# A gated recurrence followed by a low-rank mixer: 11 of ScalarE's 22 transfers go back to SyncE, and all loads and stores get new places

## The chip, the core and the metric

The kernel runs on one core of a Trainium2 chip. The core has TensorE (PE: matrix multiplications), VectorE (DVE), ScalarE (ACT), GpSimd (POOL) and SyncE (SP, which here only issues transfers). Transfers between the chip's memory and the core's on-chip memory run on 16 DMA engines; they are issued by SyncE or by ScalarE, each of which has a queue of its own. The metric is the device time of one execution in microseconds.

## What is computed

There are four batches (b), eight heads (h), 768 tokens (t) and 48 values per head (d). The first stage is a recurrence with a gate for each row of a 48 x 48 state:

```
state = zeros((B, H, D, D))
for t in range(S):
    state = alpha[:, :, t, :, None] * state + einsum('bhd,bhe->bhde', k[:, :, t], v[:, :, t])
    y[:, :, t] = einsum('bhd,bhde->bhe', q[:, :, t], state)
```

The heads of y are put side by side (8 x 48 = 384 columns), which gives x. The second stage mixes x over the tokens by a product of rank 32, adds, and goes through two layers with 1536 hidden values:

```
h  = xt @ U @ V                       # xt: tokens last
u  = x + h.transpose(0, 2, 1)
ch = maximum(u @ w_ch1, 0.0) @ w_ch2
return u + ch
```

Inputs and output are float32.

## The kernel before

**Tiling.** Each batch is worked in six chunks of 128 tokens; "1.2" is chunk 2 of batch 1. A recurrence over a chunk is turned into products: the logarithm of alpha (ScalarE, lines 378 and 549), its running sum (TensorE, 387 to 394 and 556 to 558), the exponentials of that sum and of its negative (ScalarE, 401 to 403, 566 to 569: `aa`, `ai`, `tot`), k and q multiplied by them (GpSimd or VectorE, 409 and 577, into `rkq`), both transposed (TensorE, 426 and 590, evicted into `kqt`), scores, a mask on VectorE (461, 628, into `pm`), a state product that is added to the running state (`st`, VectorE 499, 513, GpSimd 652), and y (TensorE 523 to 533, 680 and 685). v is cast to bf16 into `rv` by the helper of lines 274 to 280, on ScalarE (276), VectorE (278) or GpSimd (280). In batch 3 the transposes of k and q are DMA transposes (602), issued like a load.

The mixer of a batch follows its six chunks: the product with U (700), with V (714), the addition (VectorE, 715), transposes of u (TensorE 734, or DMA transposes 720 for batches 2 and 3), the first layer (763, 288 matmuls of 384 columns over the kernel) with its relu on ScalarE (773) or VectorE (775) into `h1t`, the second layer (789), the last addition (VectorE, 795) and the stores (798 for halves, 800 for the rest). While TensorE works on one batch's layers, the chunks of the next are prepared beside it.

**Loads.** The four inputs of a chunk go into four of 40 buffers `io`. The six chunks of batch 0 and the first four of batch 1 are loaded in token pairs: a transfer (line 348) brings 256 tokens of four heads in rows of 384 bytes. All other chunks are loaded whole (line 355): 128 tokens of eight heads in rows of 192 bytes. Both move 192 KB. The weights come as seven transfers (line 318) into the second half of the hidden layer's buffers, and are cast from there to bf16 (`w_sb`, 276 and 280).

**The order.** Every operation is recorded in a plan as a function with its buffers. Then two strings decide everything: `TABLE` has three characters for each operation, two for its number and one for the engine (P, A, D, G, or S for SyncE), and the operations are issued in that order; "++" stands for a number of matmuls that only keep TensorE busy. `SLOTS` has one character for each buffer that is taken, and names which of its pool it is. Each engine goes through its own operations strictly in this order. For a load, a DMA transpose or a store, the letter picks the queue:

```
def queue(eng):
    return nc.scalar if eng == "ACT" else nc.sync
```

A transfer also takes the next of eight completion lanes (DMAHW0 to DMAHW7 in turn, whichever engine issues it), and its engine waits before it until the transfer eight places earlier in the table has landed. This wait stands in the issuing engine's own order: what comes behind it there, computing or issuing, waits too.

Of the kernel before, what the change touches and what calls it, by code (L numbers as in the profile page):

```python
# [29 lines left out]
B1SJyABtSBqSJEPB5SBmSJFAIgPKKGJ2GI1AI+PI-AKIAIyPI4PKsAI5AIzAJGPIhDI6PI7AJ0AJzAImPIqPKHAIrAInAKaAJKPIwPKDGJ+PJHAIkPKbAKuP  # L30
BoSKwAJIPLDPJLDKcAKMPJ-DLWAJAPJJAIuPKyAJBAKfGIlDKeDKvAIxDKJGLGAI2PI3DLHAIvAIcPLEALIGIdAIePIfAKgPKiDJ3PBxSIoPJ5DLFAIpANFA
KxAIsPKhPItAJ4PKODKjAKSPKTDKLPJSPJTPJ6DK0GCISJ7PLJGKNAKUGKtGB-ACDSJ9DKkPKlDKPPKRDJUPLYPBuSLZANHPKmDNJANKAKYGFqPFrPNNGKzG
LKPCHSI8PNLAJ8DNIAKQDKnPB3ABySB7ALaALcGKqPLMALLPB6SLbDKoDKpGLNAFsPK2PLdPK4DI9AKVPFtDK8PLfAK9DKrAJCPJDAK1PK3DLePNMGLgAK+G
KAPKWANOSCEAJkPCASKBDJVDNWALOPLPDK5PK6DLhPOMAJlPB2SLQDK7DLCGLRPLSDLTGJmPCBSNYPOOPORALXAN6ANbANoANcAJePLjDLUPLiDNaAK-PLAD
LVDJpPLkPJfPLlACCSNZANPPB4ANeGLmPLnAN8PN9ANGGN-ANQDJqPLvPLtPN+ANRDOAANdGJrPLwDOQALqPLuDLxSLrDNXAOeALoPJYPLpDJMPLsSB+SNSP
NTDJgPJZPL0PL1DNfSB8ACFAJhDJsDJaPNqPNtALyPLzDL2SJbDJNPJOPNsAJnDJPDOUGNjPNkDN7AL5PMNPNUPL6ANVDL3PNrAMDPMEAB9SNvDMOAL4ANlG
MFPOBDL9PMHPMIAOPAL-PMAAOCDODSNuAMGAOgPOhAL+AMLPMJPMKDMBPOTGOiANwDMbPMTPCJAMUAL7PJRSMcDNxSMfPMPPMCAMgDNpAMMAMVPMWDMXPMYD
OHPOSAOEPMhPOFDOjGL8DMjPMkAN1PN2DOVSOGDCGAOkGMdPMRPCKSMSDMZPMQDMeDMnPN3GOIDOKPOlSOJGMoPMiAOWPJQSOLANyPMaAFuSOXDNgPNzDFpS
JoSNhDFoSJXSNAPNBPMpPONAN0DOZPJcSOmPNiDN4PM2POaDM3PGASOYDN5AOcPOdANmPMlPObGOnDOfGOoDNnDOpPOqAMxPOrPOsAMyPMqDMmDM4PO3PO4D
OyPO5PO0PO1DM7POtPNCPOzDM8PM9PF1SM5DO6DOuDJdSO2SO7SMzPM+DOvPOwDMsPMtPMuPPiPNDDPkPFvSPoPPpAPaPPbAPcPPWPPXDPdDM0DOxSPMPPNA  # L40
PCPM6SPDDPlAPgPJtSPjAPePPAPJjSPGPPhDPOPPYPPBANESPKPPLDPSPPTAPUPPVDMvDO8PF6SMrSO9APEPPPDPHAPqPPrDPIPO+PJiSPZAQFPPfDQGPGBS
QKPM1SM-SF7SPmPP7PJWSP8PPnDFjSMwSQLPF0SPFAFiSO-DPxPQHPPJDPQPPRDP2PP3PP4PP5DP6SQMPQNDQOSPsPPyPPzPQIDQJSP0DP1SPtPP9PP+DPuP
QAPQBPPvDQCPP-SPwSQDDQES
# [811 lines left out]
```

## Time and profile before

| | |
|---|---|
| median of 3 runs | 159.58 us (159.46 to 161.48) |
| the profiled execution | 159.54 us |
| its span, first instruction to last | 157.6 us |
| TensorE busy | 147.8 us (94%) |
| VectorE busy | 107.9 us (68%) |
| ScalarE busy | 90.2 us (57%) |
| GpSimd busy | 61.5 us (39%) |
| moved by DMA | 31.63 MB, mean 201 GB/s |
| transfers issued by ScalarE | 22: 7 of k, 5 of v, 5 of q, 4 of alpha, 1 of weights |
| TensorE's granted clock | full in all 40 slices |

Times in the profile count from the start of the span, in microseconds. A row of a timeline has start, busy time, engine, line, operation, what it writes <- what it reads, shapes, and the number of like instructions in a row; in brackets stands how long its engine was idle before it, and what ended that. ACTq and SPq are the issuing of transfers by ScalarE and SyncE: such a row's length is what the issue took, not the transfer. DMA in the chain of waits is the time from an issue to its landing. Tile names lose their numbers in the profile. What TensorE's share of 94% hides is where its idle time lies; that is read by stretch.

### The profile page before, as it was taken

The page shows a single profiled execution, that of the slowest core. Times are in us where ns is not written, and L with a number is a line of the kernel's source. Part 1 is how long each engine was busy: PE and PEld are TensorE (multiplying, and loading weights), DVE is VectorE, ACT ScalarE, POOL GpSimd, SP SyncE. Part 2 cuts the span into 40 slices and gives each one's busy share as a digit, 9 for nine tenths or more (in the row PEclk, how much of TensorE's full clock was granted, in tenths as well). Part 3 has the DMA queues.
Part 4 walks back from the last instruction along what each step waited for, and adds up shares of the span by engine and source line. Part 5 has one row for each costly group of instructions (what it writes and reads, how often), then busy time and mean ns, then how long its engine had stood idle before and what let it go on. Part 6 is the DMA issues. An engine that isn't in the chain of part 4 may idle for free.

```text
span 157.6 us, 4405 instructions
## 1 busy us (share of the span) xinstructions
PE 147.8 (94%) x1712; PEld 97.4 (62%) x1712; DVE 107.9 (68%) x236; ACT 90.2 (57%) x233; POOL 61.5 (39%) x95
## 2 busy tenths in 40 slices
PE   0798999998999999999999999999999999999992
PEld 0376677764766656656768666666667555666561
DVE  6029999978899538916587987875989480673162
ACT  3698799986778263999947585279232202450000
POOL 8276993556375550046578343225323000000000
PEclk9999999999999999999999999999999999999999
DMA  5999999998999999999999999979866248842044
GB/s 131 311 319 322 319 227 261 367 251 218 245 339 195 271 176 216 185 190 207 192 217 223 167 196 224 128 157 187 160 123 187 67 85 209 268 132 59 0 152 147
DMA packets 99091, 31.63 MB, mean 201 GB/s; under 512 B 92768, under 2 KB 99040, under 8 KB 99072
## 3 DMA queue, kind: packets, MB, share of 16 engines
q1 hardware_dynamic: 81312, 26.45, 74.8%
q10 hardware_dynamic: 17760, 4.92, 13.9%
q8 instruction: 13, 0.21, 0.6%
q14 instruction: 6, 0.05, 0.1%
HBM read 23.89 MB, written 4.72 MB: 181 GB/s over the span
## 4 chain that ended last, share of the span: by engine, by line
PE 83%; DMA 8%; DVE 5%; ACT 2%; issue 0%; SPq 0%; DVEq 0%
PE ps L789 30%; PE ps L763 30%; DMA io<-in_alpha_dram 5%; DMA io<-in_v_dram 3%; PE ps L714 3%; PE ps L618 3%; PE ps L590 2%; PE ps L685 2%; PE ps L556 2%; DVE pm L461 2%; PE ps L734 1%; PE ps L680 1%; PE ps L641 1%; PE ps L533 1%; PE ps L426 1%; DVE rkq L409 1%
## 5 line engine op out<-in xcount | busy, mean ns | idle before, releaser
L789 PE MATMUL ps<-w_sb,h1t 128*128 128x384 bf16 (+2 forms) x300 | 53.1, 319 | 0.0
L763 PE MATMUL ps<-uT,w_sb 128*128 128x384 bf16 x288 | 51.0, 326 | 0.1
L773 ACT ACTIVATE h1t<-ps 128x384 bf16<-128x384 f32 x58 | 27.2, 509 | 19.0 <-PE ps L763 18.8
L763 PEld LDWEIGHTS <-w_sb 128*128 128x128 bf16 x288 | 27.0, 98 | 16.4 <-issue 0.2
L789 PEld LDWEIGHTS <-h1t 128*128 128x128 bf16 x300 | 27.3, 97 | 15.9 <-issue 0.6
L775 DVE TENSOR_SCALAR h1t<-ps 128x384 bf16<-128x384 f32 x38 | 20.1, 553 | 20.1 <-PE ps L763 20.0
L628 DVE TENSOR_TENSOR pm<-ps,maskc 128x512 bf16<-128x512 f32 x28 | 17.7, 684 | 2.8 <-PE ps L618 2.8
L577 POOL TENSOR_TENSOR rkq<-io,aa 128x384 bf16<-128x384 f32 x12 | 11.3, 949 | 20.4 <-ACT h1t L773 12.1
L715 DVE TENSOR_TENSOR ub<-xb,ps 128x384 bf16<-128x384 bf16 x24 | 12.3, 550 | 6.8 <-PE ps L714 6.8
L795 DVE TENSOR_TENSOR io<-ub,ps 128x384 f32<-128x384 bf16 (+2 forms) x25 | 12.9, 533 | 3.7 <-PE ps L789 3.6
L276 ACT CAST xb<-ps 128x192 bf16<-128x192 f32 (+1 forms) x21 | 8.4, 399 | 10.5 <-PE ps L685 8.2
L461 DVE TENSOR_TENSOR pm<-ps,maskp 128x512 bf16<-128x512 f32 x20 | 13.2, 682 | 0.4 <-ACT ai L401 0.2
L652 POOL TENSOR_TENSOR st<-sm,tot 128x384 bf16<-128x384 f32 x8 | 6.6, 829 | 12.0 <-DVE sm L668 12.0
L577 POOL TENSOR_TENSOR rkq<-io,ai 128x384 bf16<-128x384 f32 x9 | 8.5, 945 | 6.7 <-ACT ai L566 3.8
L409 POOL TENSOR_TENSOR rkq<-io,ai 128x384 bf16<-128x384 f32 x9 | 9.0, 1006 | 5.4 <-ACT ai L401 3.8
L276 ACT COPY kqt<-ps 128x512 bf16<-128x512 bf16 x18 | 10.4, 610 | 1.1 <-PE ps L426 1.1
L566 ACT ACTIVATE ai<-ps 128x384 bf16<-128x384 f32 x14 | 7.0, 502 | 4.3 <-PE ps L556 2.5
L280 POOL CAST w_sb<-h1t 128x384 bf16<-128x384 f32 x14 | 7.1, 528 | 5.3 <-DMA h1t<-in_moe_w_ch_dram 5.3
L278 DVE COPY kqt<-ps 128x512 bf16<-128x512 bf16 x18 | 7.4, 418 | 1.9 <-PE ps L590 1.2
L569 ACT ACTIVATE tot<-ps,off 128x4 f32<-128x4 f32 x22 | 5.6, 279 | 5.2 <-PE ps L558 3.4
L387 PE MATMUL ps<-lt,upto 128*128 128x384 bf16 x10 | 3.6, 363 | 5.2 <-ACT lt L378 5.1
L409 POOL TENSOR_TENSOR rkq<-io,aa 128x384 bf16<-128x384 f32 x7 | 6.7, 957 | 4.1 <-DMA io<-in_q_dram 4.1
(108 smaller groups left out, 225.5 us busy)
## 6 DMA issues: line engine op xcount, KB each, us to landing
io<-in_alpha_dram SPq DMA_DIRECT2D x20, 192.0 KB, 4.6
io<-in_v_dram SPq DMA_DIRECT2D x19, 192.0 KB, 4.8
io<-in_q_dram SPq DMA_DIRECT2D x19, 192.0 KB, 4.3
io<-in_k_dram SPq DMA_DIRECT2D x17, 192.0 KB, 4.4
out_dram<-io SPq DMA_DIRECT2D x13, 192.0 KB, 2.0
h1t<-in_moe_w_ch_dram SPq DMA_DIRECT2D x4, 576.0 KB, 7.5
out_dram<-io SPq DMA_DIRECT2D x20, 96.0 KB, 2.2
h1t<-in_moe_w_ch_dram SPq DMA_DIRECT2D x2, 768.0 KB, 7.1
```

Of the source, the lines that this page charges most:

```text
L276: nc.scalar.copy(dst, src)
L278: nc.vector.tensor_copy(dst, src)
L409: eng.tensor_tensor(jh(dst()[:, :, 0:D]), raw(a), jh(x()), op=ALU.mult)
L461: nc.vector.tensor_tensor(dst, s2, maskp.to_broadcast([C, 2, 2, C]), op=ALU.mult)
L577: eng.tensor_tensor(dst()[:, :, 0:D], a(), x(), op=ALU.mult)
L628: nc.vector.tensor_tensor(pm()[:, :, par, :], s2, maskc.to_broadcast([C, HP, C]), op=ALU.mult)
L715: P.add(f"u {b}.{c}", lambda e, c=c, hb=hb: nc.vector.tensor_tensor(ub()[:, c, :], xb()[:, c, :], hb()[:, 0:DM], op=ALU.add), r=[hb] + xk( ...
L763: nc.tensor.matmul(hb()[:, 0:TW], lhsT=w1_sb[:, ct, jt * 128 : (jt + 1) * 128], rhs=u_half(uT, ct, tt, b in QUEUE_U), start=(ct == 0), sto ...
L773: nc.scalar.activation(dst, hb()[:, 0:TW], AF.Relu)
L775: nc.vector.tensor_scalar_max(dst, hb()[:, 0:TW], 0.0)
L789: nc.tensor.matmul(hb()[:, 0 : hi - lo], lhsT=h1()[:, jt, c * C : (c + 1) * C], rhs=w2_sb[:, jt, lo:hi], start=(jt == 0), stop=(jt == NJ - 1),
L795: P.add(f"out_{hi - lo} {b}.{c}", lambda e, hb=hb, lo=lo, hi=hi: nc.vector.tensor_tensor(flat(ou)[:, lo:hi], ub()[:, c, lo:hi], hb()[:, 0 ...
```

## The change

Only the two strings differ. Their first lines, before and after:

```diff
 TABLE = """
-ArSABSAvAA3SA-SQPAAySAsACLAAtSAwSCNPAzSAuACOACPA++BCiADSA++BECA++BCRGCSG++BAxSBDSCjABASCQAA4A++BCkPClACmAA7S++BDUPDVAA5S
+ArAABSAvSA-AA3SQPAAySAsSCLACNPAtSAzAA5ACOACPAAwS++BCiADSA++BECAAxS++BBAACRGAuSCSG++BCjACQA++BCkPA4SClACmA++BA7ADUPDVADWA
...
 SLOTS = """
-ABCDEFAGHAIJAABCAAKLAMANBBBOCCPCQBDRBEASBFAGHACBBDTCUAEBCBVBDGWAEACDBCGXEBAYDCACZBGAFaBHACAEbCCCFDCBHDCcdDBeBAfGgDAhHFDD
+ABCDEFAAGHIAAJBCAKLAMAABNBBOCCCPBDBEAQBFARSGHACBBDTCUAEBCBVBDGAWEACXDBCEGABDCACBEAFAYZHACAFCCCaGDCAHDCbcDdBAAefghEDAGHDD
...
```

The computing operations stand in the same order on TensorE, VectorE, ScalarE and GpSimd, on the same engines. The 154 transfers stand in another order, and fall differently on the two queues: ScalarE issued 22 and now issues 11, all of them token-pair loads (alpha of 0.0, 0.5, 0.2 and 0.4, q of 0.3 and 0.4, k of 0.5, 1.0 and 1.3, v of 0.5 and 1.3); SyncE issued 132 and now issues 143. Buffers of `io`, `rkq`, `kqt` and banks are dealt out anew.

ScalarE at its start, before. `lt` is a logarithm (of 0.0, 0.1, 0.3 and 0.5 in this order), `ai` and `aa` are exponentials (of 0.0, then 0.1), `rv0_173<-io4_137` is the cast of 0.1's v, the transfers are 0.0's v and 0.3's k:

```order
L378 ACTIVATE lt0_76<-io0_133 128x8x48
L348 DMA io9_142<-in_v_dram 128x4x96
L401 ACTIVATE ai0_181<-ps_212 128x384
L402 ACTIVATE aa0_178<-ps_212 128x384
L378 ACTIVATE lt1_77<-io1_134 128x8x48
L378 ACTIVATE lt2_78<-io2_135 128x8x48
L378 ACTIVATE lt0_76<-io3_136 128x8x48
L276 CAST rv0_173<-io4_137 128x384
L403 ACTIVATE tot0_184<-ps_212 128x8
L348 DMA io13_146<-in_k_dram 128x4x96
L401 ACTIVATE ai1_182<-ps_212 128x384
L402 ACTIVATE aa1_179<-ps_212 128x384
```

The same place after; the transfers are 0.2's alpha, 0.3's q and, ahead of the cast, 0.5's k:

```order
L378 ACTIVATE lt0_76<-io0_133 128x8x48
L348 DMA io7_140<-in_alpha_dram 128x4x96
L348 DMA io8_141<-in_q_dram 128x4x96
L401 ACTIVATE ai0_181<-ps_212 128x384
L402 ACTIVATE aa0_178<-ps_212 128x384
L378 ACTIVATE lt1_77<-io1_134 128x8x48
L378 ACTIVATE lt2_78<-io3_136 128x8x48
L378 ACTIVATE lt0_76<-io2_135 128x8x48
L348 DMA io11_144<-in_k_dram 128x4x96
L276 CAST rv0_173<-io4_137 128x384
L403 ACTIVATE tot0_184<-ps_212 128x8
L401 ACTIVATE ai1_182<-ps_212 128x384
```

Before, 0.3's k took a lane that no one waited for; after, 0.5's k takes the lane of 0.2's alpha, eight places earlier in the table, and so stands on ScalarE behind that landing and ahead of the cast. The load of 0.4's alpha, on SyncE before, comes on ScalarE directly behind the second exponential of 0.1 (`aa1_179`).

SyncE around the first weights, before: the q of 1.2 (`io34`), k and q of 1.3 (`io35`, `io36`), and the k of 1.2 (`io37`):

```order
L318 DMA h1t1_74<-in_moe_w_ch1_dram 128x3x384 x2
L348 DMA io34_167<-in_q_dram 128x4x96
L318 DMA h1t1_74<-in_moe_w_ch1_dram 128x3x384
L348 DMA io35_168<-in_k_dram 128x4x96
L348 DMA io36_169<-in_q_dram 128x4x96
L348 DMA io37_170<-in_k_dram 128x4x96
L355 DMA io39_172<-in_alpha_dram 128x8x48
L318 DMA h1t1_74<-in_moe_w_ch1_dram 128x3x384
```

After: the k of 1.2 (`io34`) is the first behind the two weights, and the q of 1.2 and 1.3 (`io36`, `io37`) come behind the third weight and 1.4's alpha:

```order
L318 DMA h1t1_74<-in_moe_w_ch1_dram 128x3x384 x2
L348 DMA io34_167<-in_k_dram 128x4x96
L318 DMA h1t1_74<-in_moe_w_ch1_dram 128x3x384
L355 DMA io35_168<-in_alpha_dram 128x8x48
L348 DMA io36_169<-in_q_dram 128x4x96
L348 DMA io37_170<-in_q_dram 128x4x96
L318 DMA h1t1_74<-in_moe_w_ch1_dram 128x3x384
```

The k of 1.3 went to ScalarE, the v of 1.2 from ScalarE to SyncE, behind the last of these rows.

SyncE in batch 3, before: `io17` and `io24` are v and q of 3.2, `io35` is v of 3.5; L602 are the DMA transposes of chunks 3.1, 3.3, 3.2, 3.4 and 3.5 in this order, L720 those of batch 2's u:

```order
L720 DMA_TRANSPOSE uT2_211<-ub2_206 128x6x128 x2
L355 DMA io17_150<-in_v_dram 128x8x48
L602 DMA_TRANSPOSE kqt3_191<-rkq3_82 128x8x128
L720 DMA_TRANSPOSE uT2_211<-ub2_206 128x6x128
L355 DMA io24_157<-in_q_dram 128x8x48
L602 DMA_TRANSPOSE kqt1_189<-rkq1_80 128x8x128
L798 DMA out_0_dram<-io21_154 64x384
L602 DMA_TRANSPOSE kqt2_190<-rkq2_81 128x8x128
L602 DMA_TRANSPOSE kqt0_188<-rkq0_79 128x8x128
L355 DMA io35_168<-in_v_dram 128x8x48
L602 DMA_TRANSPOSE kqt1_189<-rkq3_82 128x8x128
```

After, from the last transpose of batch 2's u on: q and v of 3.2, the transposes of 3.3 and 3.4, q of 3.5, the transposes of 3.1 and 3.2, v of 3.4, the transpose of 3.5, a store, v of 3.5:

```order
L720 DMA_TRANSPOSE uT2_211<-ub2_206 128x6x128
L355 DMA io31_164<-in_q_dram 128x8x48
L355 DMA io32_165<-in_v_dram 128x8x48
L602 DMA_TRANSPOSE kqt3_191<-rkq1_80 128x8x128
L602 DMA_TRANSPOSE kqt1_189<-rkq0_79 128x8x128
L355 DMA io13_146<-in_q_dram 128x8x48
L602 DMA_TRANSPOSE kqt2_190<-rkq3_82 128x8x128
L602 DMA_TRANSPOSE kqt0_188<-rkq2_81 128x8x128
L355 DMA io23_156<-in_v_dram 128x8x48
L602 DMA_TRANSPOSE kqt3_191<-rkq1_80 128x8x128
L798 DMA out_0_dram<-io17_150 64x384
L355 DMA io36_169<-in_v_dram 128x8x48
```

The transposes of 3.1 and 3.2 went behind those of 3.3 and 3.4, the v of 3.5 behind the transpose of its own chunk, and q of 3.5 and v of 3.4, which ScalarE issued, stand among them.

More of the change, by code (lines that the diff above doesn't have):

```diff
@@ L52 @@
+aFBGCBCCAeFAGCCBFEEDBCAGABAAdEHDABfADGCgCEFBDhiHkACCGFECDAABmDHClnDDADGCEFBAACBCADBFGCCjAAHDABCBEFBAAGCDACCEDCBFHEFGHJBG
+CACEDBFAABBBDGEKBACMDBCADCBAFBBDDFAGAEACOBFBLCADIPCCAGBFDAQVGecDCGZSfgCUhACABAGBAAHCFCBCBABBFDGCHBFBADCNCBAGDDCFAHEBBDCB
+ABADXCCAHDDEBkGAAHFCBDAEGHAFBEABCCEGHEBaAACGBEAAmjBCFdGAAEBDiAEDABHGFEDBDEDBECHGFBDAFECCnBGEJ
 """
```

59 lines of the change are left out of this document (28 added, 31 removed).

## The prediction

> **What bounds the kernel now.** I read the busy time of each engine by stretch first, because a share over the whole span mixes stages. The columns are start:end, length, then busy time and instruction count of PE, PEld, DVE, ACT, POOL.
>
> ```profile
> 13.06:31.39 18.33, 17.34 (x404) 13.12 (x402) 17.81 (x42) 16.55 (x45) 12.99 (x19) 1.00 1.06 298
> 32.15:39.98 7.83, 7.13 (x50) 4.23 (x49) 6.24 (x11) 6.03 (x15) 4.43 (x7) 1.00 0.93 228
> 39.98:154.67 114.69, 114.62 (x1155) 74.45 (x1154) 77.90 (x155) 58.81 (x154) 35.44 (x49) 1.00 0.87 178
> 154.67:157.62 2.95, 0.00 (x0) 0.00 (x0) 0.30 (x1) 0.00 (x0) 0.00 (x0) 1.00 0.35 122
> ```
>
> From 39.98 on TensorE idles 0.07 us in 114.69, at a granted clock of 1.00. A change that only moves transfers can win at most those 0.07 us there; it can lose any amount. From 32.15 to 39.98 TensorE idles 0.70. Before 32.15 it waits for VectorE, which idles only 0.52 us (18.33 - 17.81) between 13.06 and 31.39. So the time is the moment at which the matmul of 39.98 starts, plus 114.69 + 2.95 + 1.92; the last is the profiled execution's own 159.54 less its span of 157.62. That execution stands 0.04 under the median of 159.58.
>
> Next the chain of waits at its start (start, length, what):
>
> ```profile
> 0.74 3.56 DMA io<-in_alpha_dram
> ...
> 4.33 4.25 DMA io<-in_v_dram
> ...
> 8.59 0.37 SPq L348
> ...
> 9.00 4.07 DMA io<-in_alpha_dram
> ...
> 13.09 0.53 ACT lt L378
> ```
>
> The start is a ladder of load, freed lane, issue, load, logarithm. Transfers of both queues share eight completion lanes in program order, and each waits at its issuing engine for the transfer eight places before it: SyncE stands at 8.59 until the load issued at 4.33 has landed at 8.58.
>
> **The change part by part.** The order of computing instructions on TensorE, ScalarE, VectorE and GpSimd stays. What moves is transfers, and with them the waits.
>
> *1. ScalarE's start.* ScalarE's timeline before:
>
> ```profile
> 7.83 0.51 ACT L276 CAST rv<-io 128x384 bf16<-128x384 f32 x1
> 8.24 0.18 ACT L403 ACTIVATE tot<-ps 128x8 f32<-128x8 f32 x1
> 8.75 0.49 ACT L401 ACTIVATE ai<-ps 128x384 bf16<-128x384 f32 x1 [0.33 <-PE ps L394]
> ```
>
> In the changed program ScalarE meets the load of 0.5's k just ahead of the copy that started at 7.83, and that load takes the lane of 0.2's alpha, which ScalarE issues beside its first logarithm, as it issued 0.0's v at 4.33 before. By that row it lands at 8.58. What a ScalarE blocked by its own transfer does next is shown once:
>
> ```profile
> 83.25 0.37 ACTq L355 DMA_DIRECT2D io<-in_alpha_dram  x1
> 83.67 0.49 ACT L567 ACTIVATE aa<-ps 128x384 bf16<-128x384 f32 x1 [1.32 <-DMA io<-in_k_dram]
> ```
>
> 0.42 us from issue to the next computing instruction. So the copy starts at 8.58 + 0.42 = 9.00 instead of 7.83, 1.17 late. The exponential of 8.75 stood 0.92 behind it, 0.33 of that waiting for TensorE; without that wait 9.00 + 0.59 = 9.59, and ScalarE is about 0.8 late. Its work then has no gap until the next row:
>
> ```profile
> 13.09 0.52 ACT L378 ACTIVATE lt<-io 128x384 bf16<-128x384 f32 x1 [0.41 <-DMA io<-in_alpha_dram]
> ```
>
> This logarithm waited 0.41 for 0.4's alpha, issued at 9.00 by SyncE; now ScalarE issues it, behind that exponential's twin, at about 9.1 to 9.6, with one or two transfers more ahead of it, so the logarithm too is 0.4 to 0.8 late. VectorE begins with a multiplication that waits for 0.1's q:
>
> ```profile
> 10.75 1.20 DVE L409 TENSOR_TENSOR rkq<-io,aa 128x384 bf16<-128x384 f32 x1 [6.55 <-DMA io<-in_q_dram]
> ```
>
> It keeps its place, since 0.1's q has as many transfers ahead of it as before. The next that count:
>
> ```profile
> 12.80 0.34 DVE L499 TENSOR_TENSOR st<-ps,tot 128x192 bf16<-128x192 f32 x1
> 13.06 1.27 DVE L461 TENSOR_TENSOR pm<-ps,maskp 128x512 bf16<-128x512 f32 x2
> ```
>
> The addition of 12.80, behind the v copy and TensorE's state product, and the masks behind it inherit 0.8. From there VectorE works almost without a gap; its 0.52 idle can give back at most that. The start of the mixer's matmuls therefore moves by between 0.8 - 0.52 = +0.3 and +0.8, and I take +0.5. If the load lands early enough, this is 0.
>
> The Trainium skill, page "DMA: Bandwidth & Descriptors", section "Queues, rings and completion order", says that a DMA engine goes round-robin between the queue rows that have work, a packet at a time. By that, ScalarE's short row would overtake SyncE's backlog. The rows of 4.33 do not settle it: the load took 4.25 against 3.56 for the very first one. I price it below as a rival.
>
> *2. Chunk 1.2's k is loaded earlier.* It was issued in the second of these rows of SyncE's queue, and moves to about the place of the first:
>
> ```profile
> 24.72 0.49 SPq L348 DMA_DIRECT2D io<-in_q_dram  x1
> ```
>
> ```profile
> 28.95 3.00 SPq L348 DMA_DIRECT2D io<-in_k_dram  x1
> ```
>
> GpSimd, VectorE and TensorE around the 0.70 us:
>
> ```profile
> 34.93 0.51 POOL L280 CAST w_sb<-h1t 128x384 bf16<-128x384 f32 x1 [1.70 <-DMA h1t<-in_moe_w_ch_dram]
> 36.72 1.13 POOL L409 TENSOR_TENSOR rkq<-io,ai 128x384 bf16<-128x384 f32 x1 [1.28 <-DMA io<-in_k_dram]
> 37.81 1.23 POOL L409 TENSOR_TENSOR rkq<-io,aa 128x384 bf16<-128x384 f32 x1
> ```
>
> ```profile
> 36.99 1.27 DVE L409 TENSOR_TENSOR rkq<-io,aa 128x384 bf16<-128x384 f32 x1
> 38.19 1.26 DVE L409 TENSOR_TENSOR rkq<-io,ai 128x384 bf16<-128x384 f32 x1
> ```
>
> ```profile
> 39.51 0.40 PE L426 MATMUL ps<-ident,rkq 128*128 128x128 bf16 x4 [0.63 <-DVE rkq L409]
> ```
>
> GpSimd's two and VectorE's two multiplications run at the same time, and VectorE's take 1.26 each. The same shapes without a partner:
>
> ```profile
> L577 DVE TENSOR_TENSOR rkq<-io,ai 128x384 bf16<-128x384 f32 x5 | 3.3, 672 | 0.1
> L577 DVE TENSOR_TENSOR rkq<-io,aa 128x384 bf16<-128x384 f32 x2 | 1.1, 546 | 0.0
> ```
>
> 0.67 and 0.55: side by side they lose 0.59 + 0.72 = 1.31 us. The load moves some 4.2 us forward; by its old distance from issue to use (28.95 to 36.72) it is there at 32.5. GpSimd can then start at 35.44, when its cast ends, 1.28 earlier, and is through the first multiplication before VectorE starts its pair. Its second, until about 37.6, still covers some 0.6 of VectorE's first. Half of the 1.31 is enough: VectorE's second must end before 38.88 (39.51 - 0.63) rather than at 39.45. The gap before 39.51 closes: -0.63, and with the 0.07 behind it -0.70. If 1.3's q, which GpSimd's second needs, comes a microsecond late, the overlap comes back and so does the gap.
>
> *3. The middle.* ScalarE no longer waits for transfers (the 1.32 at 83.25). TensorE idles 0.07 in all there, so I cost this at 0; the cover is TensorE's queue. SyncE takes these issues, at about 0.6 each.
>
> *4. Batch 3.* The loads that ScalarE issued, 3.5's q and 3.4's v among them, now stand in SyncE's queue among the transposes, and a transpose waits there for its operands with all behind it. The rows before, of SyncE, then of GpSimd and TensorE, and how long a whole-chunk load took there:
>
> ```profile
> 108.25 2.63 SPq L602 DMA_TRANSPOSE kqt<-rkq  x2
> 110.94 0.58 SPq L355 DMA_DIRECT2D io<-in_v_dram  x1
> 115.06 1.24 SPq L602 DMA_TRANSPOSE kqt<-rkq  x1
> ```
>
> ```profile
> 120.73 0.50 POOL L280 CAST rv<-io 128x384 bf16<-128x384 f32 x1
> ```
>
> ```profile
> 122.18 0.36 PE L685 MATMUL ps<-rv,pm 128*128 128x48 bf16 x8
> ```
>
> ```profile
> DMA to landing us min/median/max: 3.0/3.3/3.6
> ```
>
> 3.5's v was issued at 110.94; now it comes behind 3.5's transpose and one store (0.6): 115.06 + 1.24 + 0.6 = 116.9. Landing 119.9 to 120.5, copied by 121.0, wanted at 122.18: 1.2 us of margin, cost 0. The transposes of 3.1 and 3.2 move behind those of 3.3 and 3.4: about where 108.25 shows a pair, so issued by 111, landed by 114.6 at the same 3.6, and wanted by the scores at 115.83:
>
> ```profile
> 115.83 0.78 PE ps L618 x24
> ```
>
> Cost 0, margin 1.2. The final stores and the 2.95 behind the last matmul stay.
>
> **Sum.** 159.54 + 0.5 - 0.70 + 0 + 0 = 159.3.
>
> **The rivals.**
>
> *A: ScalarE is not held up.* If 0.2's alpha lands by about 7.4 (7.83 less 0.42), nothing moves at the start and only -0.70 is left: 158.8. If VectorE also loses its 0.52 of idle, since several of its operands load earlier, 158.3. For it: the load has only the backlog of the first seven transfers ahead of it. Against it: 0.0's v in the same place landed at 8.58. This is where the skill's round-robin would lead; the 4.25 speaks rather against it.
>
> *B: the gap at 39.51 stays.* GpSimd's second multiplication waits for 1.3's q, now behind a weight load and two others, and collides with VectorE's pair again. Then 159.54 + 0.5 = 160.0, and 160.3 with the full 0.8.
>
> *C: slower, by SyncE's queue in batch 3.* One place: 3.5's v behind the transpose of 3.5. If that transpose leaves 1 us later than 115.06, because its rows wait for a buffer that an earlier, now later, transpose frees, and the load takes 4.8, the median of all SyncE's v loads (row below), it lands at 122.7, is copied by 123.2, and TensorE waits 1.0: 160.3. It decides from 1.2 us of lateness on; past 2% (162.8, 3.3 above the median) it takes 4.7.
>
> ```profile
> io<-in_v_dram SPq DMA_DIRECT2D x19, 192.0 KB, 4.8
> ```
>
> *D: nothing moves.* ScalarE's transfers cost it nothing before and cost SyncE nothing now: 159.5. The Trainium skill says so in the same page, section "Issuing engines are not separate DMA queues": issuing from several engines saves only the sequencer's time. The trace speaks against it as a whole: at 8.59 and 83.25 an engine stands in order behind its own transfer's lane.
>
> **How the numbers follow.** The forecast 0.45, A 0.20, B 0.13, C 0.14, D 0.08. The predicted time is the forecast's, 159.3 us. The range takes in A's 158.3, the forecast's own 159.1 to 159.6, B, and the first two microseconds or so of C: 158.1 to 161.0; left out are the far ends of A (0.06) and C (0.10). A measurement of this kernel tells about 2% from no change, so faster means under 156.4 and slower over 162.8. Faster would need more than the 0.70 + 0.52 of idle that the stretches hold, so the first 13 us would have to shorten by two: 0.04. Slower is half of C: 0.07. Within 2%: 0.89.
>
> **What would show it.** ScalarE's timeline: a transfer of k issued at about 8.6 and the copy behind it near 9.0 (step 1); if the copy is at 7.8, A. VectorE's masks at 13.06 should come 0.3 to 0.8 later. GpSimd's multiplication of 1.2's k should start near 35.5, VectorE's pair should take under 1.9 together, and TensorE's transpose of 1.3 should show no wait (step 2). From there to the last matmul TensorE should idle under 0.2 in about 114.7 (steps 3 and 4); idle time in front of L685, L680 or L618 between 105 and 123 is C. The prediction is wrong if the stretch behind the start of the mixer's matmuls grows, or if VectorE starts later than 10.75, which I cost at nothing.

## The result: 158.67 us against 159.55, and the profile after

| | before | after |
|---|---|---|
| median, 16 runs each | 159.55 us (158.54 to 161.48) | 158.67 us (158.10 to 159.58) |
| ratio | | 0.9934, 95% interval 0.991 to 0.9958 |
| the profiled execution, and its span | 159.54, 157.6 | 158.11, 156.1 |

The change makes the kernel faster by 0.66% (0.42 to 0.90), about 1.05 us. The profiled execution after is one of the quick ones: the two profiles differ by 1.43 us, more than the ratio says. What follows splits these 1.43 us first, and asks the experiments how much of them is typical.

TensorE's stretches after, cut at the same instructions as before (the mixer's first matmul, and the matmul behind the transpose of 1.3):

```profile
31.91:38.69 6.78, 6.78 (x51) 4.25 (x48) 5.23 (x11) 4.82 (x12) 3.89 (x6) 1.00 1.08 274
38.69:153.15 114.46, 114.42 (x1158) 74.31 (x1155) 78.18 (x155) 59.73 (x156) 35.22 (x48) 1.00 0.83 176
```

These lengths run from start to start, so they hold waits that the busy times beside them do not show as idle. The start is 0.24 us shorter (31.91 against 32.15), the stretch around the gap 1.05 (6.78 against 7.83, and without any idle time), the long stretch 0.23 (114.46 against 114.69), the tail the same 2.95; what lies outside the span is 0.09 longer. -0.24 - 1.05 - 0.23 + 0.09 = -1.43.

The chain of waits at the start, after, and ScalarE's timeline at the places that the prediction named:

```profile
0.74 3.08 DMA io<-in_alpha_dram
...
3.85 4.24 DMA io<-in_alpha_dram
...
8.10 0.37 ACTq L348
```

```profile
8.52 0.51 ACT L276 CAST rv<-io 128x384 bf16<-128x384 f32 x1 [1.05 <-DMA io<-in_alpha_dram]
...
13.02 0.52 ACT L378 ACTIVATE lt<-io 128x384 bf16<-128x384 f32 x1
```

ScalarE does stand behind its own load of 0.2's alpha, for 1.05 us, and is held as computed: the load takes 4.24 us (4.25 was taken), and the cast follows its landing by 0.44 (0.42). But the whole ladder begins 0.48 us earlier, because the first load takes 3.08 us instead of 3.56. So the cast is at 8.52 and not at 9.00, and the logarithm of 0.4 at 13.02, where it was. VectorE's masks come 0.16 later than before:

```profile
13.22 1.29 DVE L461 TENSOR_TENSOR pm<-ps,maskp 128x512 bf16<-128x512 f32 x2
```

Around the gap, after, on GpSimd, VectorE and TensorE:

```profile
33.50 0.91 POOL L409 TENSOR_TENSOR rkq<-io,ai 128x384 bf16<-128x384 f32 x1
35.47 0.91 POOL L409 TENSOR_TENSOR rkq<-io,aa 128x384 bf16<-128x384 f32 x1 [1.05 <-ACT w_sb L276]
37.01 0.65 POOL L280 CAST w_sb<-h1t 128x384 bf16<-128x384 f32 x1 [0.63 <-DMA h1t<-in_moe_w_ch_dram]
```

```profile
36.75 0.55 DVE L409 TENSOR_TENSOR rkq<-io,aa 128x384 bf16<-128x384 f32 x1
37.22 0.86 DVE L409 TENSOR_TENSOR rkq<-io,ai 128x384 bf16<-128x384 f32 x1
```

```profile
38.47 0.39 PE L426 MATMUL ps<-ident,rkq 128*128 128x128 bf16 x4
```

GpSimd's pair starts 3.2 us earlier than before and is done before VectorE's begins; VectorE's pair takes 0.55 and 0.86 instead of 1.27 and 1.26 (the second overlaps the cast of a weight on GpSimd at 37.01); TensorE's transpose of 1.3 waits for nothing.

### The profile page after: what moved, and what is told of

The parts are those of the page before. It is cut to its first block, busy times and chain, and to the rows that moved or that the text cites. A ratio compares the mean times of both kernels' runs of the same rounds, so it can differ in the third digit from the quotient of the medians.

```text
span 156.1 us, 4408 instructions
## 1 busy us (share of the span) xinstructions
PE 146.8 (94%) x1712; PEld 97.3 (62%) x1712; DVE 106.7 (68%) x236; ACT 90.0 (58%) x233; POOL 61.7 (39%) x95
## 4 chain that ended last, share of the span: by engine, by line
PE 84%; DMA 5%; DVE 4%; ACT 4%; issue 1%; ACTq 0%; DVEq 0%
PE ps L789 31%; PE ps L763 30%; DMA io<-in_alpha_dram 5%; PE ps L714 3%; PE ps L618 3%; DVE pm L461 2%; PE ps L590 2%; PE ps L685 2%; PE ps L556 2%; PE ps L426 2%; PE ps L450 1%; PE ps L680 1%; PE ps L734 1%; PE ps L533 1%; PE ps L641 1%; ACT aa L402 1%
## 5 line engine op out<-in xcount | busy, mean ns | idle before, releaser
L763 PE MATMUL ps<-uT,w_sb 128*128 128x384 bf16 x288 | 51.0, 326 | 0.0
L763 PEld LDWEIGHTS <-w_sb 128*128 128x128 bf16 x288 | 27.0, 98 | 16.1 <-issue 0.2
L577 POOL TENSOR_TENSOR rkq<-io,aa 128x384 bf16<-128x384 f32 x12 | 11.6, 974 | 22.9 <-ACT aa L567 11.7
L409 POOL TENSOR_TENSOR rkq<-io,ai 128x384 bf16<-128x384 f32 x9 | 8.5, 945 | 6.1 <-DMA io<-in_k_dram 3.0
L577 POOL TENSOR_TENSOR rkq<-io,ai 128x384 bf16<-128x384 f32 x9 | 8.2, 913 | 6.1 <-DMA io<-in_q_dram 3.9
L278 DVE COPY kqt<-ps 128x512 bf16<-128x512 bf16 x18 | 7.4, 419 | 1.5 <-PE ps L590 1.0
L409 POOL TENSOR_TENSOR rkq<-io,aa 128x384 bf16<-128x384 f32 x7 | 6.4, 910 | 2.9 <-ACT aa L402 1.8
```

Of the source, the lines that this page charges most:

```text
L278: nc.vector.tensor_copy(dst, src)
L409: eng.tensor_tensor(jh(dst()[:, :, 0:D]), raw(a), jh(x()), op=ALU.mult)
L577: eng.tensor_tensor(dst()[:, :, 0:D], a(), x(), op=ALU.mult)
L763: nc.tensor.matmul(hb()[:, 0:TW], lhsT=w1_sb[:, ct, jt * 128 : (jt + 1) * 128], rhs=u_half(uT, ct, tt, b in QUEUE_U), start=(ct == 0), sto ...
```

## The experiments

Twelve kernels, each built from one of the two by moving entries of the table or changing an entry's engine letter. In the diffs S stands for SyncE and A for ScalarE. Each ratio is to the kernel before, run on the same chip beside it (medians 159.62 to 159.68 us there), with its 95% interval.

### 1. The gap alone: 1.2's k moved in the kernel before

```diff
 S wload1 1
+S load 1.2 k
 S load 1.2 q
 S wload1 3
 S load 1.3 k
 S load 1.3 q
-S load 1.2 k
```

> The kernel before, with one transfer moved: the load of 1.2's k stands directly ahead of 1.2's q on SyncE instead of behind 1.3's q; nothing else differs. Theory (the gap before TensorE's transpose of 1.3 is the whole gain): GpSimd's multiplication of 1.2's k starts by 35.5 instead of 36.72, VectorE's pair takes under 1.5 us together instead of 2.46, the transpose shows no wait, and the time falls by 0.9 to 1.2 us, to about 158.5. The prediction's own figure for this step is -0.70 (158.9). Rival (the gain comes from the start, or from taking transfers off ScalarE): within 0.3 us of the kernel before.

Measured: 159.32 us, ratio 0.9972 (0.9942 to 1.0002), about -0.45 us, not told from nothing. GpSimd, VectorE and TensorE around the gap:

```profile
36.13 0.91 POOL L409 TENSOR_TENSOR rkq<-io,ai 128x384 bf16<-128x384 f32 x1
37.01 1.03 POOL L409 TENSOR_TENSOR rkq<-io,aa 128x384 bf16<-128x384 f32 x1
```

```profile
37.19 1.27 DVE L409 TENSOR_TENSOR rkq<-io,aa 128x384 bf16<-128x384 f32 x1
38.37 0.55 DVE L409 TENSOR_TENSOR rkq<-io,ai 128x384 bf16<-128x384 f32 x1
```

```profile
38.98 0.40 PE L426 MATMUL ps<-ident,rkq 128*128 128x128 bf16 x4
```

The transpose shows no wait any more; counted against the transpose of 1.2 just ahead, it comes 0.68 us sooner, the prediction's figure. But GpSimd starts at 36.13, not 35.5, since the third part of the weights now lands at 35.61 and its cast stands ahead; so one of VectorE's two still collides. And 0.23 of the 0.68 is given back at the next transposes, those of 1.5, whose k GpSimd waits for. That row, before and here:

```profile
50.49 0.99 POOL L577 TENSOR_TENSOR rkq<-io,ai 128x384 bf16<-128x384 f32 x1 [0.97 <-DMA io<-in_k_dram]
```

```profile
50.44 0.91 POOL L577 TENSOR_TENSOR rkq<-io,ai 128x384 bf16<-128x384 f32 x1 [1.46 <-DMA io<-in_k_dram]
```

The load does not move when the gap closes, so a second place, which had 0.24 us to spare in the profile before, becomes the limit. "The gap is the whole gain" is too simple.

### 2. The gap put back: 1.2's k moved back in the changed kernel

```diff
-S load 1.2 k
 S wload1 3
 S load 1.4 alpha
 S load 1.2 q
 S load 1.3 q
+S load 1.2 k
```

> The changed kernel, with 1.2's k put back behind 1.3's q on SyncE; nothing else differs. Theory: the gap of 0.6 us before the transpose of 1.3 is back, and the time rises by 0.9 to 1.2 us over the changed kernel, so that it stands within 0.4 us of the kernel before. Rival (the start or ScalarE's relief made the gain): it keeps at least half of the gain, so 158.9 or less.

Measured: 159.37 us, ratio 0.9988 (0.9957 to 1.0018): the gain is gone, as the theory had it for the time (the interval just touches that of the changed kernel, 0.991 to 0.9958). Not as it had it for the row:

```profile
35.92 0.91 POOL L409 TENSOR_TENSOR rkq<-io,ai 128x384 bf16<-128x384 f32 x1 [2.33 <-ACT w_sb L276]
36.79 1.02 POOL L409 TENSOR_TENSOR rkq<-io,aa 128x384 bf16<-128x384 f32 x1
```

```profile
36.97 1.26 DVE L409 TENSOR_TENSOR rkq<-io,aa 128x384 bf16<-128x384 f32 x1
38.15 0.55 DVE L409 TENSOR_TENSOR rkq<-io,ai 128x384 bf16<-128x384 f32 x1
```

In the profiled execution (158.57 us) the load lands at 35.76, half of the collision returns, and TensorE loses 0.53 us against the changed kernel, though the profile shows a wait of only 0.12 in front of the transpose of 1.3. The median lies 0.8 us above that execution, so others lose more; which wait does it there no profile shows.

### 3. The first load's company

```diff
-S load 0.0 alpha
+A load 0.0 alpha
 S load V
-A load 0.1 alpha
+S load 0.1 alpha
```

> The kernel before, with two letters changed: 0.0's alpha is issued by ScalarE and 0.1's alpha by SyncE, behind the small load of V, so that the first load shares the DMA engines with 96 KB instead of 192. Theory: 0.0's alpha lands near 3.8 instead of 4.30, all of ScalarE's start comes 0.48 earlier, VectorE starts near 10.1, and the mixer's matmuls start 0.2 to 0.5 earlier; the time falls by 0.2 to 0.5. Rival (VectorE's later work or the landing of later loads sets the start, so nothing passes through): within 0.1 of the kernel before, with the first landing earlier all the same. Second rival (the 0.48 was chance of one execution): the first load lands near 4.3.

Measured: 159.24 us, ratio 0.9991 (0.9955 to 1.0027), not told from nothing, nor from the 0.2 to 0.5 us expected. The first load in the chain of waits:

```profile
0.73 2.95 DMA io<-in_alpha_dram
```

It is no chance. In the six profiles in which 0.0's and 0.1's alpha, 192 KB each, are issued together, the first lands at 3.91 to 4.38 us (mean 4.2); in the eight in which the small load of V (96 KB) goes beside it, at 3.54 to 3.82 (mean 3.66). The two groups also differ in the engine that issues the first load (SyncE in the six, ScalarE in the eight); no run separates the two. The mixer's first matmul comes 0.33 us earlier than before. In the profiled execution, which lies 1.1 us above the median, TensorE then waits at both thin places for GpSimd:

```profile
38.82 0.40 PE L426 MATMUL ps<-ident,rkq 128*128 128x128 bf16 x4 [0.50 <-POOL rkq L409]
...
49.55 0.40 PE L590 MATMUL ps<-ident,rkq 128*128 128x128 bf16 x4 [0.79 <-POOL rkq L577]
```

In this execution 1.2's k lands at 37.70 and 1.5's at 51.42, both later than before, with the same orders behind the start. The first of these waits is no longer than the 0.63 of before; the second is new. An earlier start is worth nothing in an execution in which these loads set the time; what it is worth in the others the interval does not say.

### 4. The hold taken away

```diff
 (the changed kernel)
-A load 0.5 k
+S load 0.5 k
```

> The changed kernel, with one letter changed: the load of 0.5's k is issued by SyncE at the same place of the table, so that ScalarE does not stand behind the landing of 0.2's alpha before its cast of 0.1's v. Theory (the hold is real and its 0.7 us pass on through VectorE's masks): the cast starts near 7.4 instead of 8.52, the masks near 12.5 instead of 13.22, and the mixer's matmuls start 0.3 to 0.7 earlier; the time is 0.3 to 0.7 under the changed kernel. Rival (VectorE's start is set by the landing of 0.1's q and by what its queue holds, so the hold is hidden): the cast is earlier, and the time the same within 0.15.

Measured: 158.28 us, ratio 0.9919 (0.9892 to 0.9946). ScalarE's cast and VectorE's masks, then the scores of batch 3 on TensorE:

```profile
7.17 0.51 ACT L276 CAST rv<-io 128x384 bf16<-128x384 f32 x1
```

```profile
12.71 1.29 DVE L461 TENSOR_TENSOR pm<-ps,maskp 128x512 bf16<-128x512 f32 x2
```

```profile
114.68 0.62 PE L618 MATMUL ps<-kqt 48*128 48x128 bf16 x16 [0.40 <-DMA kqt<-rkq]
```

The cast is 1.35 us earlier, the masks 0.51, the mixer's first matmul 0.55 (31.36 against 31.91). The hold is real, and costs here what the prediction took for it (+0.5). In the profiles of 7 and 12, which leave the hold out too, the masks also start early (12.81 and 12.61), but the mixer's first matmul stands at 31.88 and 32.01, so how much arrives there varies. It is the quickest version with a full set of runs, 0.4 us under the changed kernel by the medians, but the two intervals overlap. In the profiled execution batch 3 returns 0.48: the transpose of 3.2 took 5.06 us from issue to landing, where the changed kernel's took 3.13.

### 5. The letters alone: ScalarE's late transfers given to SyncE

```diff
 (the kernel before; the same places)
-A load 1.5 q, 2.0 v, 2.1 v, 3.3 alpha, 3.1 alpha, 3.2 alpha, 3.4 k, 3.1 k, 3.2 k, 3.4 q, 3.5 q, 3.4 v; wload2 1
+S load 1.5 q, 2.0 v, 2.1 v, 3.3 alpha, 3.1 alpha, 3.2 alpha, 3.4 k, 3.1 k, 3.2 k, 3.4 q, 3.5 q, 3.4 v; wload2 1
```

> The kernel before, with 13 letters changed: the 12 whole-chunk loads and the one weight load that ScalarE issues from 35 us on are issued by SyncE at the same places of the table. Theory (TensorE idles 0.07 us there, so ScalarE's waits are covered, and SyncE has room for the issues): the same time as before within 0.3 us, with TensorE's idle time behind 40 us still under 0.2. Rival (issuing from SyncE alone makes a DMA transpose of batch 3 or a load late): 0.5 us or more slower, with TensorE idle in front of L618, L680 or L685. Other rival (ScalarE's relief is what the change gains): 0.5 us or more faster.

Measured: 160.60 us, ratio 1.0058 (1.0024 to 1.0092), 0.9 us slower. TensorE's waits, and GpSimd's behind the second:

```profile
38.52 0.40 PE L426 MATMUL ps<-ident,rkq 128*128 128x128 bf16 x4 [0.68 <-POOL rkq L409]
...
49.66 0.40 PE L590 MATMUL ps<-ident,rkq 128*128 128x128 bf16 x4 [1.21 <-POOL rkq L577]
...
117.79 0.84 PE L618 MATMUL ps<-kqt 48*128 48x128 bf16 x24 [0.70 <-DMA kqt<-rkq]
```

```profile
48.70 0.91 POOL L577 TENSOR_TENSOR rkq<-io,aa 128x384 bf16<-128x384 f32 x1 [1.85 <-DMA io<-in_q_dram]
```

The rival holds. This execution lies 0.8 us above the median. Its first wait stands in front of 1.2's transposes instead of 1.3's, and is about as long as the 0.63 of before; the other two are new. 1.5's q, issued by ScalarE at 35.77 before, now stands in SyncE's queue behind the lanes and a weight load: issued at 40.96, landed at 48.54 instead of 41.27. In batch 3 the transposes of 3.2 and 3.4 stand behind 3.2's k, 3.4's q and 3.5's q, which joined the queue; they leave 3.6 us later than before by the clock (2.4 more than TensorE is late by then) and take 5.0 and 4.6 us. So the part of the change that its description names first, taken alone, loses; the new places have to make up for it.

### 6. The margin of 3.5's v

```diff
 (the changed kernel)
-S load 3.5 v
 S store 0.0
 S store 0.1
 S store 0.2
+S load 3.5 v
```

> The changed kernel, with the load of 3.5's v moved behind three more stores in SyncE's queue, so that it is issued some 2.0 us later, near 117.4. By the prediction's step 4 and rival C the margin is about 1.2 to 1.5 us: it lands near 120.6, is copied by 121.1, TensorE waits about 0.5 us in front of y of 3.5 (L680 or L685 near 120.5), and the time rises by 0.4 to 0.6 over the changed kernel. Rival (the transfer is quicker with fewer around it, or the margin is larger): no wait and the same time.

Measured: 158.61 us, ratio 0.9955 (0.993 to 0.9979). GpSimd's cast and TensorE's y of 3.5:

```profile
120.15 0.50 POOL L280 CAST rv<-io 128x384 bf16<-128x384 f32 x1 [1.04 <-DMA io<-in_v_dram]
```

```profile
120.33 0.33 PE L680 MATMUL ps<-st,kqt 128*128 128x96 bf16 x4
120.71 0.36 PE L685 MATMUL ps<-rv,pm 128*128 128x48 bf16 x8
```

The load was issued at 117.22, landed at 120.10 (2.9 us, quicker than the 3.2 assumed), and is now the last to arrive: L685 follows L680 by 0.38 instead of 0.17. So 1.5 us later costs 0.2 there, and the time does not rise by the 0.4 to 0.6 expected (the two profiles end 0.04 apart, as this one had gained 0.16 ahead of that place). The margin is as large as the prediction had it; rival C's place is not the weak one.

### 7. Batch 3 without 3.4's v beside the transpose

```diff
 (the kernel of 4)
+S load 3.4 v
 S load 3.5 q
 S transposes 3.1, 3.2
-S load 3.4 v
```

> The kernel in which SyncE issues 0.5's k, with 3.4's v moved ahead of 3.5's q, so that it does not run beside the transpose of 3.2 (in the profile of that kernel the transpose took 5.06 us instead of 3.13 beside the load, and the scores waited 0.40). Theory (start 0.5 earlier by the missing hold, and the wait in batch 3 a collision that this takes away): the transpose of 3.2 lands by 113, no wait over 0.1 in front of L618, and 0.5 to 0.8 us under the changed kernel, so 157.9 to 158.2. Rival (the long transpose was chance, not the load): the time of the kernel without this move, near 158.3.

Measured: 158.32 us, ratio 0.9933 (0.9904 to 0.9963): nothing gained. The transposes of 3.1 and 3.2 took 5.3 and 4.5 us in the profiled execution, although the load (issued at 107.81, landed at 110.92) was gone from beside that of 3.2, issued at 110.83, and the scores waited again:

```profile
115.38 0.62 PE L618 MATMUL ps<-kqt 48*128 48x128 bf16 x16 [0.29 <-DMA kqt<-rkq]
```

So 3.4's v is not what makes 3.2's transpose long. Transposes of 4.5 us and more there appear in five profiles of fourteen (4, 5, 7, 11 and 12), and what makes them long stays open.

### 8. The third part of the weights

```diff
 (the kernel of 1)
-A load 1.2 v
 S wload1 2
+S load 1.2 v
```

> The kernel before, with 1.2's k ahead of 1.2's q as in the earlier run, and 1.2's v moved from ScalarE to SyncE behind the last part of the first weights. Theory (what that earlier run lacked of the changed kernel's gain is the third part of the weights, whose cast stands ahead of GpSimd's multiplications: 35.6 there, 33.0 in the changed kernel): the third part lands by 35.0, GpSimd's pair is done or nearly done when VectorE's begins, both of VectorE's take under 0.7 us, and the time is 0.8 to 1.1 us under the kernel before (158.6). Rival (the rest of the gain lies in the start or elsewhere): the same as with 1.2's k alone, 0.3 to 0.5 under the kernel before.

Measured: 159.42 us, ratio 0.9991 (0.9959 to 1.0023). The third part landed at 35.42, only 0.2 sooner than in 1 (in an execution in which the first two parts landed 0.8 later than there), and the transpose of 1.5 waited:

```profile
52.00 0.40 PE L590 MATMUL ps<-ident,rkq 128*128 128x128 bf16 x4 [0.59 <-POOL rkq L577]
```

A miss in the landing and in the time. GpSimd's pair is nevertheless done (37.72) when VectorE's begins (37.86), both of VectorE's take 0.55, and from the mixer's first matmul to the one behind 1.3's transposes TensorE takes 6.79 us, as after (6.78). The place that binds next is again 1.5. The profiled execution lies 1.1 us above the median.

### 9 and 10. The second place: the weight load's queue in the kernel before

```diff
 (the kernel of 1: experiment 9; the kernel before: experiment 10)
 S load 1.5 k
-A wload2 1
+S wload2 1
```

> The kernel before with two edits: 1.2's k ahead of 1.2's q, and the one weight load that ScalarE issues (768 KB, directly behind 1.5's k in the table) issued by SyncE at the same place. Theory (a second thin place: in the kernel before 1.5's k lands at 50.35, 8.6 us after its issue, beside ScalarE's weight load, and its transpose at 51.7 has 0.24 us to spare; so closing the gap at 39.5 alone opens a wait there): 1.5's k lands by 48.5, no wait in front of the transpose of 1.5, and the time is 0.6 to 1.0 us under the kernel before (158.7 to 159.0). Rival (the weight load's queue does not matter): 1.5's k lands at 50 or later, and the time is that with 1.2's k alone, 0.3 to 0.45 under.

> The kernel before with only the weight load's letter changed. Theory (the second place only binds when the first is closed): 1.5's k lands by 48.5, the gap at 39.5 stays, and the time is that of the kernel before within 0.3 us. Rival (the weight load's queue is a gain by itself): 0.5 us or more faster.

Measured: 158.54 us, ratio 0.9963 (0.9927 to 0.9998) with both edits, about 0.6 us by the ratio (five of the twelve runs lie at 159.0 to 160.3); 159.48 us, ratio 1.0002 (0.9972 to 1.0033) with the letter alone. With both, on TensorE by stretch and on GpSimd:

```profile
31.80:38.80 7.00, 6.93 (x49) 4.13 (x47) 5.53 (x11) 5.04 (x13) 2.76 (x4) 1.00 0.97 255
```

```profile
48.29 0.92 POOL L577 TENSOR_TENSOR rkq<-io,ai 128x384 bf16<-128x384 f32 x1
```

1.5's k lands at 47.43 instead of 50.35, and GpSimd no longer waits for it; no transpose waits. Two entries of the table give the median of the changed kernel, and 1.13 of its 1.43 us between profiles (158.41); by the ratios they are not told apart, and the interval of both edits also overlaps that of the first alone. With the letter alone 1.5's k lands at 48.81, not by 48.5 as expected, the time is that of the kernel before, and there are waits at both places:

```profile
38.22 0.40 PE L426 MATMUL ps<-ident,rkq 128*128 128x128 bf16 x4 [0.21 <-POOL rkq L409]
...
49.26 0.40 PE L590 MATMUL ps<-ident,rkq 128*128 128x128 bf16 x4 [1.10 <-DVE pm L628]
```

The second wait here is for 1.5's q multiplication, behind a weight cast on GpSimd (that weight landed at 47.77).

### 11. The weight load's queue in the changed kernel

```diff
 (the changed kernel)
 S load 1.5 k
-S wload2 1
+A wload2 1
```

> The changed kernel with that weight load issued by ScalarE again, at the same place of the table. Theory: ScalarE's row shares the DMA engines with SyncE's, 1.5's k lands at 48.5 to 50 instead of 46.5, the transpose of 1.5 (0.87 us to spare in the changed kernel) waits 0.3 to 1 us, and the time rises by 0.3 to 1.0 over the changed kernel. Rival (the load of 1.5's k is set by its place, not by the other queue): it lands near 46.5 and the time is the same.

Measured: 158.66 us, ratio 0.9945 (0.9921 to 0.997), the time of the changed kernel. 1.5's k lands at 46.03, and GpSimd does not wait for it:

```profile
48.74 0.91 POOL L577 TENSOR_TENSOR rkq<-io,ai 128x384 bf16<-128x384 f32 x1
```

A miss. The letter moves the landing in the old order and not in the new. In the old order the part of the weights ahead of 1.5's k lands at 45.97 and ScalarE's load is issued 0.8 us behind the k; here the part lands at 42.80 and the load is issued 1.6 us behind. Whether one of these is the reason stays open; no run changes one alone.

### 12. More margin in batch 3

```diff
 (the kernel of 4)
 S transpose 3.3
+S load 3.5 q
 S transpose 3.4
-S load 3.5 q
-S transpose 3.1
 S transpose 3.2
+S transpose 3.1
```

> The kernel in which SyncE issues 0.5's k, with SyncE's order in batch 3 changed: 3.5's q directly behind the transpose of 3.3, and the transpose of 3.2 directly behind that of 3.4, then that of 3.1. Two profiles without the hold showed transposes of 3.1 and 3.2 that took 4.5 to 5.3 us instead of 3.1 to 3.5, whatever load ran beside them, and 0.3 to 0.4 of waiting for scores. Theory (such slow transposes happen in some executions, and the changed order leaves only 1.8 us for 3.2): with 3.2 issued near 107.5 and 3.1 near 108.8 both have over 2.2 us to spare, no execution shows a wait in front of L618, and the time is 0.5 to 0.8 under the changed kernel (157.9 to 158.2). Rival (the waits in batch 3 are rare, or the start's gain is given back elsewhere): 158.3, as without this edit.

Measured: 158.23 us (157.59 to 160.88, 6 runs), ratio 0.9915 (0.9882 to 0.9949): not told from 158.28. Its one profile is of the execution of 160.88, and is no witness for the others; there, too, a transpose (3.1) took 4.97 us, and at 1.5 TensorE waited longer than in any other profile:

```profile
49.56 0.40 PE L590 MATMUL ps<-ident,rkq 128*128 128x128 bf16 x4 [1.26 <-POOL rkq L577]
```

In that execution 1.5's k landed at 49.62, so the changed order does not keep this place free in every execution. Whether the order helps stays open.

### The two thin places over the profiles

TensorE's idle time in front of the transposes of chunks 1.2 and 1.3, and of 1.5, and what landed before them (us):

| kernel | 1.2's k | third weights | wait, 1.2 and 1.3 | 1.5's k | wait, 1.5 |
|---|---|---|---|---|---|
| before | 36.56 | 34.88 | 0.63 | 50.35 | 0 |
| 3, first load | 37.70 | 36.01 | 0.50 | 51.42 | 0.79 |
| 5, letters alone | 36.97 | 34.36 | 0.68 | 49.52 | 1.21 |
| 10, weight letter | 36.78 | 33.69 | 0.21 | 48.81 | 1.10 |
| 1, 1.2's k | 32.82 | 35.61 | 0 | 50.31 | 0.06 |
| 8, and 1.2's v | 33.34 | 35.42 | 0 | 50.89 | 0.59 |
| 9, 1.2's k and weight letter | 31.60 | 34.32 | 0 | 47.43 | 0 |
| after | 31.10 | 32.98 | 0 | 46.52 | 0 |
| 2, 1.2's k late | 35.76 | 33.03 | 0.12 | 47.19 | 0 |
| 12, in its slowest run | 33.56 | 36.38 | 0 | 49.62 | 1.26 |

The changed order has these loads 2 to 5.5 us earlier than the kernel before, and in the profiles of 4, 6, 7 and 11, which keep its order there but for the entry named, neither place shows a wait. By the profiles that is most of the gain: not one stall removed but two places with more room, where the old order had one stalled and the other 0.24 us from it. The times of the single edits are too close to each other to split it between the two.

A smaller part is not the transfers' doing. The same two matmuls on TensorE, and the mask on VectorE ahead of the second, before:

```profile
43.39 0.24 PE L558 MATMUL ps<-ones,lt 128*128 128x1 bf16 x4
43.65 0.81 PE L763 MATMUL ps<-uT,w_sb 128*128 128x384 bf16 x4
```

```profile
42.90 0.69 DVE L461 TENSOR_TENSOR pm<-ps,maskp 128x512 bf16<-128x512 f32 x1
```

After:

```profile
42.11 0.24 PE L558 MATMUL ps<-ones,lt 128*128 128x1 bf16 x4
42.21 0.81 PE L763 MATMUL ps<-uT,w_sb 128*128 128x384 bf16 x4
```

Before, the second matmul writes into a bank that this mask must have read (it ends at 43.59); after, into one that a relu of ScalarE has read, and it follows 0.10 us behind the first instead of 0.26. A matmul at 85.19 (L641) likewise no longer waits for a bank that VectorE reads. Together they are worth about 0.3 us: from 39.98 to 44.46 on the clock of before, TensorE takes 4.48 us in all seven profiles with the old banks and 4.32 or 4.33 in six of the seven with the new ones (4.70 in 11); from 52.10 to 86.49 it takes at least 34.39 with the old, and 34.23 in six of seven with the new (34.57 in 12). The profile after gives 0.08 of it back at 1.5. So this part comes from dealing out the banks anew; no run changes the banks alone.

## Why the prediction was right, and where not

**The time and its direction.** Forecast 159.3 in 158.1 to 161.0, measured 158.67; within 2%, as nine chances in ten said. The gain was about 1.05 us where the sum made 0.25; the time lies inside because the range was wide, for the start, the gap and the middle were each off to the same side.

**Step 1, ScalarE's start.** The hold was right in each piece (4.24 us for the load, 0.44 to the cast) and, in the one profile of experiment 4, in its price: 0.55 us at the mixer's first matmul for the +0.5 taken. (The lanes go round in the order of the built program, which differs a little from the table's: 0.2's alpha stands eight transfers ahead of 0.5's k there, four in the table.) What the step lacked is a term: the first load, now issued by ScalarE and with V's 96 KB beside it instead of another 192, lands about half a microsecond sooner (experiment 3; which of the two does it is open). The prediction said of VectorE's start that it "keeps its place"; it moved from 10.75 to 10.01. The two nearly cancel: VectorE's last copy ahead of the mixer (`uT`, L278) starts at 31.30 before and at 31.31 after, and over the profiles at 31.34 on average in the six with the old start, 31.37 in the four with the changed one and 30.90 in the three without the hold. So +0.5 should have been about 0. The -0.24 of the two profiles arises behind that copy, and is smaller than the scatter among the six with the old start, whose first matmul of the mixer stands at 31.69 to 32.70.

**Step 2, the gap.** The mechanism was right: GpSimd's pair ahead of VectorE's, the two pairs apart, no wait in front of the transpose. The term "-0.63, and with the 0.07 behind it -0.70" was mis-sized; the stretch shortened by 1.05. The idle time that the profile shows is not the whole wait, because the ends of matmuls are modelled: the three in front of the transpose of 1.3 (L763, at 38.23 before) count 0.65 us, while after (at 37.98) the transpose starts 0.49 behind them. From start to start, the transpose of 1.3 comes 0.79 us sooner behind the work ahead of it than before, and the matmul behind it another 0.25 (it starts 0.22 behind the transpose instead of 0.47). This second part is a wait for a relu on VectorE, which stands behind VectorE's pair; it is there without a stall at the transpose too. In experiment 1, where the transpose at 38.98 shows no wait, the relu and the next matmul on TensorE were:

```profile
38.84 0.55 DVE L775 TENSOR_SCALAR h1t<-ps 128x384 bf16<-128x384 f32 x1
```

```profile
39.44 0.65 PE L763 MATMUL ps<-uT,w_sb 128*128 128x384 bf16 x3
```

GpSimd's two multiplications went out of the way entirely, since the third weights too land 1.9 us earlier; a weight cast still met VectorE's second. How VectorE loses its time could have been read from the rows of before: its two multiplications end at 38.26 and 39.45, each 0.41 after GpSimd's (37.85 and 39.04), and in experiment 1 at 38.46, 0.42 after GpSimd's 38.04. After, the second ends at 38.08, 0.42 after the end of GpSimd's cast (37.66). It does not slow down, it waits until GpSimd's instruction has ended. The Trainium skill says this ("SBUF — State Buffer", section "SBUF: two separate sides": the port pair that the two share is an exclusive lock, held for the whole instruction), and these ends agree with it.

**Step 3, the middle.** "I cost this at 0; the cover is TensorE's queue" came out for the changed order in the sense that nothing was lost (0.04 us idle in 114.46), but its reason was wrong. Nor did its bound hold, that moving transfers "can win at most those 0.07 us there": the stretch shortened by 0.23, by waits for banks that the profile counts as busy; the banks are missing in the prediction. Little idle time in one execution says nothing of margins: the transposes of 1.5 had 0.24 us, and the same letters in the old order cost 0.9 us (experiment 5). The place was missing in the prediction, as a risk and as a source of gain.

**Step 4, batch 3.** 3.5's v landed at 118.64 in a profile that runs 1.5 us ahead, so at 120.15 on the clock of before, within the 119.9 to 120.5 of the step. The weak place is the transposes of 3.1 and 3.2 beside it, for which the step took 3.6 us at the most; they take 4.5 to 5.3 in some executions, and TensorE then idles 0.3 to 0.4 in the profiles of 4, 7 and 11 (0.70 in 5, nothing in 12).

**The rivals.** A fell by its mechanism (the cast at 8.52, not before 7.83); that its 158.8 lies closer to the time than the forecast is luck. B did not come: 1.3's q landed at 35.33. C's mechanism is seen at another place, the transposes, for less than half its price, and not in the changed kernel's own profile. D fell with experiment 5: thirteen letters alone change the time by 0.9 us. Of the Trainium skill's round-robin between queue rows ("DMA: Bandwidth & Descriptors", section "Queues, rings and completion order"), which spoke for A, the start shows nothing. The old order behind 40 us may be its work, though no run shows that: there 1.5's k, issued by SyncE at 41.77, landed at 50.35, just behind the weights that ScalarE issued 0.8 us later (50.18), and at 47.43 once SyncE issued them; experiment 11 shows that it need not come to that.

## What to carry to other kernels

Where one stage feeds a saturated engine, list for each of that engine's steps how long its last operand has been ready, and not only where it waits: closing the one gap that a profile shows (-0.68) gave part of it back at a place that had 0.24 us to spare and no idle time. A transfer's engine is a choice about waits in order: moving 13 issues from ScalarE to SyncE cost 0.9 us at unchanged places. And the idle time that a profile shows for TensorE is less than its waits: compare the starts of the same matmuls in two profiles. That finds a wait for a bank as well as one for a load, here 0.3 us that stood nowhere as idle time.

## What the runs showed of the hardware

- Two loads of 192 KB issued together land the first at 3.91 to 4.38 us; with 96 KB as the second, at 3.54 to 3.82. The first load is issued by SyncE in the one group and by ScalarE in the other, so its company is not shown to be the reason.
- A VectorE multiplication of k or q (L409, L577) that starts while GpSimd is at a multiplication or a cast ends 0.41 to 0.42 us after GpSimd's instruction: in all 64 cases in the fourteen profiles in which GpSimd's began at least 0.04 us ahead and had 0.2 us or more to go. In the 13 in which GpSimd's began less than 0.02 us ahead VectorE went first, and GpSimd's ended 0.77 to 0.78 us after VectorE's.
- The DMA transposes of 3.1, 3.2 and 3.4 took 3.1 to 3.6 us in nine profiles; in the other five, one or two of them took 4.5 to 5.3. Taking 3.4's v from beside 3.2's did not change it.
